# One kernel, 2,842 operations, another written-out order: fused sliding-window attention and gated MLP on one core

## The chip, the cores and the metric

One core of one Trainium2 chip runs the whole program. The metric is the device time of one execution in microseconds; the time of the kernel before is the median of its runs. The profile is a separate execution of the same program with the hardware profiler on; its own time is given below beside its span.

## The reference

There are 8 batches, 8 heads, 576 positions and 64 elements per head. Attention looks back over a window of 128 positions, with a bias that falls linearly with distance and a slope for each head. Its output, 4,608 tokens of 512 elements, goes through an MLP whose gate is `h * cos(h)`.

```python
scores = scale * np.matmul(q, k.transpose(0, 1, 3, 2))
bias = slopes[:, None, None] * (-np.abs(rel).astype(np.float32))[None, :, :]
mask = (rel >= 0) & (rel < window)                      # window = 128
scores = np.where(mask, scores + bias[None], -1000000000.0)
attn = softmax(scores)                                  # written out in the original
x = (attn @ v).transpose(0, 2, 1, 3).reshape(4608, 512)
h = x @ w_in                                            # 512 -> 2048
out = (h * np.cos(h)) @ w_out                           # 2048 -> 512
```

## The kernel before

**Stages.** The tokens are handled in nine chunks of 512 (the phases 0 to 8). Attention of the first batch comes ahead of them, as the opening part; the attention of the other batches is spread over the phases 0 to 5, between the matmuls of the MLP. The chunk of phase 0 is computed in two halves of 256 tokens (`moe1_half`, L975 to L984), the later ones in whole chunks (`moe1`, L782 to L791) or, from phase 6 on, by a seven-product scheme of block sums (`moe1_fast`, L876 to L943; the second matrix, L1067, uses such a scheme from phase 1 on). Those block sums are made by VectorE: `w_sums` and `w_in_sums` from the weights, `x_sums` from the tokens.

**One attention unit** is a pair of heads and 256 queries, or the 64 queries of the tail for all heads. Its steps are: `scores` (TensorE, L529 and L539), `exps` (ScalarE, L590 and L598), `mask` (VectorE, multiplies by the table `emask` of bias and window, L611 and L623), `pv` (TensorE, L640 to L656), `norm` (VectorE, a reciprocal L694 and a product L696), and `x_pe`, which transposes the result on TensorE (L742) and copies it to `xT` by ScalarE (L752) or VectorE (L753). In phases 2 to 5 some results go to `xT` by a transposing DMA instead (`x_dma`, L762 and L768, on SyncE's queue).

**The opening part.** The first 256 rows of q come by SyncE's queue into `ob` and are cast by VectorE and ScalarE (L367, L368). The first rows of k, and the second rows of both, come by Pool's queue (`load_qk`, L356). `qk_transposes` turns them on TensorE (L483): for each of q and k one block from the first rows (32 transposes for both) and one from the second rows (40 for both). Each block leaves two halves in PSUM, in two banks, and each half is copied to the tiles `qt` and `kt` by ScalarE (L500) or VectorE (L501). `masks` makes `emask`: eight exponentials on ScalarE, one for each head (L460), and four copies on VectorE (L465), each of which needs two of them.

**Later batches.** q and k of batch 1 come by `load_qk` as well. From batch 2 on `load_nat` (five DMAs each on Pool's queue, L385) brings them to `qnat` and `knat`, and `dma_transposes` (two transposing DMAs each on SyncE's queue, L396 and L399) turns them. `load_v` brings v in five blocks of rows for each batch (L375); `load_w_in` and `load_w_out` bring the weights in four parts each (L407, L413). All of these are on Pool's queue.

**What sets the order.** The program first makes a list of 2,842 operations with the tiles that they read and write. A packed table then gives one order of all of them; each engine runs its own operations in that order, and the table also names the engine for each copy that ScalarE or VectorE could do:

```python
for lo, hi in zip(raw[:n], raw[n:]):
    at = (at + lo + 256 * hi) % 65536
    o = self.all[at % 32768]
    if isinstance(o.fn, dict):
        e = "dve" if at >= 32768 else "act"
        o.fn, o.eng = o.fn[e], (e,)
    self.order.append(o)
```

Waits on semaphores follow from the list and the order (`emit`): an operation waits for the last one on each other engine or queue that it depends on. Nothing is reordered when the program runs. An operation that waits therefore holds up whatever stands behind it on its engine; on Pool and SyncE these are the issues of DMAs.

Of the kernel before, what the change touches and what calls it, by code (L numbers as in the profile page):

```python
# [8 lines left out]
ALU = mybir.AluOpType  # L9
# [21 lines left out]
    'c-nPV2Y6If7JmPfH!Wo*A%PHdEHqifjs=k}tV#(GFqBXPBn4$bu`FK_%_4*%1ObV(K#D*JSt&-E!h-'  # L31
    '0xDvPKfD@{Z`QYO7kX6D^JciMYzU|;fHUhcd1+;jf_Kj&N_3_w#jJy552L+3%Pc;zlP#H-yktj(-'
    'pEjqM{ck}PJwCrB3q-'
    '{9M;&d$5qHR9WADS}~;_2H1xbO#`q+wdtgon`B>6%HyG|f?3%VnDsdnr<5N0St5ZZ)?8zmXNGD<Zg2=y6N`U+Gy?'
    '$F$*GyJWJoN!r+3anTS_iMU&FrmJy)q1{k##U*rYHRJHq^Dy35b!Y@oPU}o$A?_9;n<O%5Xs0l2&{m^^1BgNm_9P'
    '~pqObs4C1TN&{Qy{6(86~%nA#%H5NW^O=4`d2vLnc~h(_}2&mQcz_^`@$G{b79x#rnLjt-93Hcj0-'
    'yv%|m2e+*e0cZK}!+72b)WUaJT8@pXD+fk0N6bOV1gB(Si4?NA5T2-'
    '!JB(zEKr!Mj%{>;HUNYjab!Z7$qCql;L3G!CjefR+FFk(bw73vr<2ntCbb8MB)_5dQYyf6J%<J=0tY;ul(MgN&rc'
    'O0s&EiG$uIcm#Y~Vab;v#yqnaVrE7GY>V-A}Btqa`;P_Nv&jvF#{*7WM`>VMkre&#)Wy?uO_aV#gax-'
    'm{4=v5trFP6j>R?Tw2c0rY#J*M(j<PaOY>o)>#w^hUa2)xJ2kX>J~-'  # L40
    '#3SczLYEI#)13`0UMgZCvSU&r@KXVhQx8AYHOt^~S#t385v1pL)39f1&X4(!RY_VSn%~;N7Le~0Vt5k)3C!7qncH'
    'Sb_KKyP6<WQBL=(H{om`}^2hwehkBNkN1f6-'
    '=6Jf`#n1*9F&|{#~8ip5b`?XFO3>mnmKg4fqM&X#D2BXTu`vb#MxEL-'
    '2=FZh<=U!>)?uhVjo~ev?pC0h90j^d!W2#$W>Vg}3Lez;yMB~`dF58D5!*GHZ4bkokcrZJo8XMBIs3+J`c0!*&!='
    'cNak2M(+9t6%k<c;_TI5&xT-;_~SjMe)zLQ?kr-'
    '9G)}so_oZgT~!nS)>B%(>F{i(nL<%Kma6dPT_kIY8xqVGm@6sSZY)QY;}3kyZHF!JjrNbPWohF6A1kpQae^Jz>4Y'
    'nMq|4ag_#Z%abX$X0Qx{bdg5-'
    'w!C^Sy0wzSSv6YO*7!5g5KOZPW>L)jeqDWi^PVfHiNt_&bV&I7<#pb?el1f*R3lvbBscPqQM6(|M=#E!7MQtWiEo'
    '^$q8jetWg{{laSk`ID;w6<lHL!It@CI3ZRWxET-dy=6bdfZi^BN)-'
    'kx6rkxYh^Af7Y$CX%W0qP@nf!;+_cuy#JAV$$(>L5)aS8M@n1a32RRL3Yb{W0a`!VJ8|o4{JEnxs(L});p(&v8a9'  # L50
    'u_yO{KZHL$YuW?tu(Sy-'
    '!vCGTmAdZpg4wXLtycpkG<<E5@OtDZg=!_1h1+Njmjw*z0aL)7QnhFOPv(elHPlI>oe%EXgvk}suL+RHI+l!oPEe'
    'ttc)y)KY7q-'
    'GO9HpEp~!82*s>_!_J5TR{@5f%EL7h^Wh(4l4fbO%j~jd783&`#My06C4>3;+Is6L%3tT|^hYe#$tr1&iB&6{dwW'
    'wmj!;Baz_4=p8Jja_9ps>tY{=<;GUvOwSAXGq+K`;>!KNrH|ImXY(ASTzHFN^apdvpSj*r6^VK)$8H@P=`NPcPO&'
    'XkYSBhFw`irt0gqb!LQPqlVQC7VwU?z)4yP6n<)+6xUk=rH29r)HJ=#nkkufV0J5o_@v9wsQWd0@&P$WT0e*0vOC'
    'WIl=#9la*x}LDtWaQG=0xl2(#f%Kz3QWi+K|tR$xwKh#_K~ywPUk>V_~X988-'
    'dL$7M*|kTUzrMQ~>ttJm@GYT>9QFLiQ#JGHIu^Q5UX9joXGsV+1N~s5tf4rg&Z0t843@yK)VUZ;eO{vvf>bj#_<{'
    'E{YJE13lG{)N}UY3D6Y>lsCkRX4ja{$9_e$IQETy;j`zD56VwIGwJ{vRRhIkkY72;<?OL;WxyDsbjLJ`d?#gik4L'
    '%OwvOj>3X-Yk5pe`ia}jeHouYwjx-lYe?zUO*6w~{=z!E<7?VOdoJcyIBk3;YN22T&Udsl*?z2EoT*eN`VQ(2lOw'  # L60
    '$ie!%Cd#CND}y^H-5G~apWoVM#%(x$>q1=4UeA7@v$>FHVpXpRNz-`z1w9-2S&rNI|0<^yIkuIxJ1&2qr-'
    'yn-P&*BAkwbEg<YgZWM`B<Ux7!?;yxT0hEB9Poq9_H<xB+6$<+&1*V*jXQ=!i##UhbBC-HxJ9b4f>O5FQM$GVlYY'
    '0;EzOMeT$+Oi@ir?~G>em;QF`Fb7Uw0-'
    ')DSUv5QX5E;wvHsQX@ok50m+CO*%wR0XM0gH$JNq(o?|pd}rcrfU%@Ny^NS$EwY}9WNlRrb}CwAb0!CyUIkX8zeE'
    't`lBMNi5`Z9289jS-byN0#8`Z0-K46!6u51NJvfI*I<pVOKD}#Bep<(EjKAJ>#OvyA?}aT-'
    'Eb<QtZWG>gAiq@nZu|-Z>5YIIxXgTPJ-Qv8(%8OF{x~utj?J<T~4~q=Mu!G!`B%o{U^X7EYfMjy|cFw5l`KlR}P!'
    'Ka8_mW<8uzKs|eA|5Ic*_e7cdlcU3q+K^v!GU5I4-4igxj^A<ASLge=;<iQSZL!w7=WR?W#-'
    'vXhCLeN@7x(>g+{qRDABl6lLS<Fw>!h`LQKaFe(HMu)ipAva=P&;AW;|7_8}?>Xa&1&CWqRI3oTyJm0VHkMj~b-'
    'KU~R;VLVn(IO$x|2XD-#Cwa~YvoxGM@0FUnOnlZXB(9|3jhMQu{ARUV7(DVnyPJ@o)_f&pP-'
    '0v1&I@q5tK0fHEZqW2B6vpePz;Nsr3p!)OwvLraMQ%IB0%b!Fk8kvD!^ICX(d5SU`>)JBl;A)3x!^A~*gA1H!Njk'  # L70
    '9bb31AJ#9jLnSFn5nJP8V+>6WI*{{9$K=-'
    'Ii4(}ekB>9rlTbz8;dAV@$vsGY#Mm*p3)v9cI)0mEeyn;9Sk1Ej+_{IEB=6m(OWM%qp|L4FkV=POcUwRSz4?%tjO'
    '!EE7%nJVFo1y$1xLEKDW3+%V*`a_(LEi!<eA{Ja22J?)4@RI|7PRIIN8a6UkTIrQNx^0MmIX}Gdse33v8*ibI3(}'
    'Q6!`hQq7VFL0TWDyL%1z)LEb|Fqa2QJsRyz<9M$)jGC(Gyq6mu#GUiIyWiMn}lrw_vC^2CnX65Kq(JOA5auqsW#('
    'az6gPr;3Fs3vS*iFTO!lleCE-fW~K`s@;f-'
    'DuL7*vWwMFvwo)YDYK%Ys!&lL=}a$qa_Dqe_$j$%4|P%7Sk&C^p7|E-05OoaEoQU{w(_HKhuIl)N)0L6E?If-ndQ'
    'f>bOkomPRMj6=zXYB;2Fs8S$=8>KAS9bxj%$jo92RQykW$_h$ynL-'
    ';1n|B~0C{NjJ5M;#~HD{_qDyS92ASr8Q=(}$hf?wlN8Dh7U35CEE3Rb4eZHcVrLB=YO&ys+EVM&F9-'
    '>_E|awkyN8>TE$>Y^ZLfm%hXRv?#4)t*Y5EYzr4%5w1xWK3uw7gWYn<tfyI;9|8HRZ>;#t145fwkp%W<gb}oO8Vt'
    ';%~TDI391Zd3iT@kVuEmcuME+!AOkCeh?Xh408{MGRAGcvK=>2_;SOCz;Xi5FXBMh@##BcNK~)Hu608vNLvl*BDH'  # L80
# [172 lines left out]
def bass_alibi_sliding__then__act_gcu_kernel(  # L253
# [8 lines left out]
    with ExitStack() as ctx:  # L262
# [966 lines left out]
        for u in range(1, 4):  # L1229
            load_w_in(u)  # L1230
            if u == 1:
                load_v(0, range(NBLK - LORD, NBLK))
# [92 lines left out]
```

## Time and profile before

| what | value |
|---|---|
| median of 3 runs | 299.79 us (299.76 to 300.42) |
| the profiled execution's own time | 299.71 us |
| its span in the profile | 298.0 us |
| granted TensorE clock | 1.0 |

The span reaches from the first to the last instruction of the profile; 1.71 us of the profiled execution's time lie around it. Lines beginning with a time in the quoted timelines are merged: the first number is the start, the second the length from the first to the last instruction of the group, and "x4" says how many there are.

### The profile page before, as it was taken

How to read it: one execution, taken by the hardware profiler on the slowest of the kernel's cores; microseconds unless marked ns; L12 is line 12 of the kernel's file. 1: busy time of each engine (PE TensorE's matmuls, PEld its weight loads, DVE VectorE, ACT ScalarE, POOL GpSimd, SP SyncE). 2: the span in 40 equal slices, each digit the busy share in tenths (PEclk: the TensorE clock that was granted, in tenths of full speed). 3: DMA queues.
4: the chain of work that ended last, by engine and by line, in shares of the span. 5: the costliest groups of instructions: out<-in, count | busy, mean ns of one | idle time of the engine just before them, and what ended most of it. 6: DMA issues, size and time to landing. Idle time of an engine off the chain costs nothing.

```text
span 298.0 us, 7278 instructions
## 1 busy us (share of the span) xinstructions
PE 287.9 (97%) x2974; PEld 205.2 (69%) x2974; DVE 262.1 (88%) x522; ACT 222.1 (75%) x318; POOL 95.2 (32%) x122
## 2 busy tenths in 40 slices
PE   2899999999999999999999999999999999999996
PEld 2678845446874586458854788547768888888884
DVE  3879877599977999899999999999999999999972
ACT  5788878689757889688777878579778758778620
POOL 7997000599642303991195005000000000000000
PEclk9999999999999999999999999999999999999999
DMA  7999999999999994999999939973131400041033
GB/s 153 173 205 208 207 169 146 180 196 155 136 175 147 130 187 90 142 173 173 169 170 133 163 85 130 159 164 74 21 79 21 150 2 0 2 141 37 10 134 106
DMA packets 147729, 37.96 MB, mean 127 GB/s; under 512 B 133360, under 2 KB 146416, under 8 KB 147696
## 3 DMA queue, kind: packets, MB, share of 16 engines
q0 software_dynamic: 99344, 18.10, 79.7%
q1 hardware_dynamic: 48352, 19.41, 34.5%
q8 instruction: 23, 0.38, 0.5%
q14 instruction: 10, 0.08, 0.1%
HBM read 36.70 MB, written 9.44 MB: 155 GB/s over the span
## 4 chain that ended last, share of the span: by engine, by line
PE 94%; DVE 2%; POOL 1%; issue 1%; ACT 1%; POOLq 0%; DVEq 0%
PE ps L1067 33%; PE ps L782 24%; PE ps L876 11%; PE ps L539 5%; PE ps L975 5%; PE ps L1161 4%; PE ps L653 3%; PE ps L656 2%; PE ps L742 2%; PE ps L483 2%; PE ps L529 1%; DVE kt L501 1%; PE ps L640 1%; PE ps L642 1%; PE ps L1138 1%
## 5 line engine op out<-in xcount | busy, mean ns | idle before, releaser
L1067 PE MATMUL ps<-w_outb,gT 128*128 128x256 f16 x512 | 82.3, 273 | 0.0
L782 PE MATMUL ps<-xT,w_inb 128*128 128x512 f16 x336 | 82.2, 379 | 0.0
L787 ACT ACTIVATE cos<-ps,halfpi 128x512 f32<-128x512 f32 x84 | 54.9, 687 | 18.9 <-PE ps L782 13.9
L598 ACT ACTIVATE p<-ps 128x768 bf16<-128x768 f32 (+1 forms) x64 | 55.6, 915 | 11.5 <-PE ps L539 9.5
L791 DVE TENSOR_TENSOR gT<-ps,cos 128x512 f16<-128x512 f32 x84 | 54.5, 686 | 5.5 <-ACT cos L787 5.1
L1067 PEld LDWEIGHTS ps<-w_outb,gT 128*128 128x128 f16 x512 | 48.2, 98 | 12.5 <-issue 1.3
L782 PEld LDWEIGHTS ps<-xT,w_inb 128*128 128x128 f16 x336 | 31.7, 98 | 31.1 <-DVE gT L791 1.5
L375 POOL DMA_DIRECT2D vp<-in_v_dram x40 | 34.3, 892 | 53.1 <-PE ps L656 35.3
L1067 PE MATMUL ps<-wsum,gsum 128*128 128x256 f16 x256 | 38.5, 273 | 0.0
L623 DVE TENSOR_TENSOR p<-p,emask 128x768 bf16<-128x768 bf16 (+1 forms) x64 | 38.0, 615 | 0.3
L385 POOL DMA_DIRECT2D qnat<-in_q_dram x30 | 25.5, 918 | 23.9 <-DMA qt<-qnat 23.9
L1052 ACT ACTIVATE ob<-ps 128x512 f32<-128x512 f32 x33 | 19.6, 598 | 13.7 <-PE ps L1067 11.2
L385 POOL DMA_DIRECT2D knat<-in_k_dram x30 | 25.7, 948 | 9.3 <-DMA kt<-knat 7.0
L1067 PEld LDWEIGHTS ps<-wsum,gsum 128*128 128x128 f16 x256 | 23.2, 98 | 4.0 <-issue 0.5
L876 PE MATMUL ps<-xT,w_inb 128*128 128x256 f16 x132 | 24.8, 273 | 0.0
L696 DVE TENSOR_TENSOR xnats<-ps,rec 128x256 f16<-128x256 f32 x56 | 21.9, 420 | 0.5
L539 PE MATMUL ps<-qt,kt 64*128 64x128 bf16 (+1 forms) x320 | 20.1, 253 | 1.3 <-DVE kt L501 1.3
L653 PEld LDWEIGHTS ps<-vp,p 128*128 128x128 bf16 x256 | 16.0, 99 | 4.3 <-issue 1.0
L653 PE MATMUL ps<-vp,p 128*128 128x65 bf16 x256 | 18.9, 196 | 0.1
L1067 PE MATMUL ps<-wsum,gT 128*128 128x256 f16 x112 | 18.1, 273 | 0.0
L539 PEld LDWEIGHTS ps<-qt,kt 64*128 64x128 bf16 x320 | 11.9, 98 | 8.6 <-issue 3.6
L1161 PE MATMUL ps<-w_outb,gT 128*128 128x512 f16 x64 | 17.6, 380 | 0.0
(111 smaller groups left out, 478.0 us busy)
## 6 DMA issues: line engine op xcount, KB each, us to landing
out_dram<-ob SPq DMA_DIRECT2D x35, 256.0 KB, 2.7
vp<-in_v_dram POOLq DMA_DIRECT2D x32, 128.0 KB, 6.9
qnat<-in_q_dram POOLq DMA_DIRECT2D x24, 128.0 KB, 7.1
knat<-in_k_dram POOLq DMA_DIRECT2D x24, 128.0 KB, 10.8
w_inb<-in_moe_w_in_dram POOLq DMA_DIRECT2D x4, 512.0 KB, 10.5
w_outb<-in_moe_w_out_dram POOLq DMA_DIRECT2D x4, 512.0 KB, 21.8
gsum<-in_q_dram POOLq DMA_DIRECT2D x1, 576.0 KB, 15.5
gsum<-in_k_dram POOLq DMA_DIRECT2D x1, 576.0 KB, 17.6
```

The costliest lines, as they stand in the source:

```text
L375: op("pool", [lambda e, t=t, rows=rows: e.dma_start(vp[b % 2][0:rows, t, :, 0:64], v[b, :, 128 * t:128 * t + rows, :].rearrange("h p d -> ...
L385: fns.append(lambda e, t=t, rows=rows: e.dma_start(nat[which][b % 2][0:rows, t, :, :], src[b, :, 128 * t:128 * t + rows, :].rearrange("h p ...
L539: ins = e.matmul(ps[:, banks[x], c0:c1], keys_ap(b, x, pr, kc), query_ap(b, x, pr, qb, 128 * nb), start=c0 == 0 and (b, pr, G) not in seed ...
L598: op("act", lambda e: e.activation(P[i][:, :, 0:hi], src_[:, :, 0:hi], ACTF.Exp, scale=0.125), w=held + [("P", i)], occ=920 if G else 691, ...
L623: op("dve", lambda e: e.tensor_tensor(p, p, m, ALU.mult), r=[("EM", h0), ("EM", h1)] + ([] if G else [("EM2", h1)]), w=[("P", i)], occ=600 ...
L653: ins = e.matmul(o, P[i][:, x, d0:d0 + 128], V[:, kc, h, 0:65], start=True, stop=not two)
L782: op("pe", lambda e, kc=kc: e.matmul(ps[:, bank, :], w_in[:, kc, 128 * fc:128 * fc + 128], xT[:, kc, r0:r0 + CH], start=(kc == 0), stop=(k ...
L787: op("act", lambda e: e.activation(cosb[ci][:, :], ps[:, bank, :], ACTF.Sin, bias=halfpi[:, 0:1]), r=["halfpi"], w=[("B", bank), ("cos", c ...
L791: op("dve", lambda e: e.tensor_tensor(gT[gi][:, fc, :], ps[:, bank, :], cosb[ci][:, :], ALU.mult), r=[("cos", ci)], w=[("B", bank), ("g", ...
L876: op("pe", lambda e, i=i, kc=kc: e.matmul(ps[:, bank, 256 * i:256 * i + 256], left(kc, p0 + i), right(kc), start=(start and i == 0 and kc ...
L1067: op("pe", lambda e, t=t, p=p: e.matmul(ps[:, bank, 256 * t:256 * t + 256], left(p, slice(128 * t, 128 * t + 128)), right(p), start=(start ...
L1161: op("pe", lambda e, t=t, fc=fc, bank=bank: e.matmul(ps[:, bank, :], gT[gi][:, fc, 128 * t:128 * t + 128], w_out[:, fc, :], start=(fc == 0 ...
```

## The change

The table is another one. No operation is added or taken away, none computes anything else, and the four settings and branches that are new in the text (`PCOS`, `LORD == 3`, and the choice of a group's name in `op`) are not active: `PCOS` is False and `LORD` is 0.

```diff
 TABLE = (
-    'c-nPV2Y6If7JmPfH!Wo*A%PHdEHqifjs=k}tV#(GFqBXPBn4$bu`FK_%_4*%1ObV(K#D*JSt&-E!h-'
...
+    'c-nPV30ze57M^bwhFMr<7^T$QEz8o<a>=as{FPaT3#KNbB8pE%)AtN2H6bm0F1e(MlA2-)YA7zzs`;`q$t-'
...
 )
-        f = fn[0] if isinstance(fn, list) else fn["act"] if isinstance(fn, dict) else fn
+        f = fn[0] if isinstance(fn, list) else next(iter(fn.values())) if isinstance(fn, dict) else fn
...
+        PCOS = False
...
-                op("dve", lambda e: e.tensor_tensor(o, srcs, cos, ALU.mult),
-                   r=r + ck, w=w + gk(hf), occ=1139, lat=1225, pri=MPRI, two=hf == 1)
+                f = lambda e: e.tensor_tensor(o, srcs, cos, ALU.mult)
+                if hf and PCOS:
...
+                else:
+                    op("dve", f, r=r + ck, w=w + gk(hf), occ=1139, lat=1225, pri=MPRI,
+                       two=hf == 1)
...
+        if LORD == 3:
...
+        else:
             distances()
             identity()
             load_qk("q", q, 0, 1)
```

Unpacked, the two tables give these orders. Of the operations on each engine, this many stand at another place in its sequence: 1,497 of 1,860 on TensorE, 115 of 304 on ScalarE, 326 of 522 on VectorE, 49 of 70 on Pool, 60 of 86 on SyncE. Fourteen copies change their engine, seven each way.

```
Pool, opening part (b0, b1: batches; "rows 2": the second rows of batch 0)
before: k rows 1 | distances 1 | q rows 2 | distances 2, 3 | k rows 2 | identity 1, 2 |
        v b0: 1, 0, 3 | w_in 0 | v b0: 2 | w_in 1, 2, 3 | q b1, k b1 | v b0: 4 | w_out 0-3
after:  k rows 1 | q rows 2 | distances 1 | identity 1 | distances 2 | identity 2 | k rows 2 |
        distances 3 | v b0: 1, 0, 3, 2 | w_in 0, 1, 2, 3 | v b0: 4 | q b1, k b1 | w_out 0-3

ScalarE, opening part (E: an exponential of masks, by head)
before: E2 E6 | cast q | E3 E0 E1 E5 | q copy a | k copy a | E4 E7 | exps 0, 1 | q copy d |
        exps 2, 3 | exps 4 5 6 | x copies 0, 2, 3 | exps tail, 7 | x copy 5 | cosines ...
after:  cast q | E6 | q copy a | E3 E1 E7 E0 E4 E5 E2 | exps 0, 1 | q copies c, d |
        exps 2, 3 | exps 4 5 6 | x copies 1, 2, 3 | exps tail, 7 | cosines ...

VectorE, opening part (a, b: halves of the first block, c, d: of the second)
before: memsets | cast q | q copy b | emask copy | k copy b | emask copies x3 | mask 0, 1 |
        q copy c | k copies d, c | mask 2, 3 | norms 0, 1 | norms 2, 3 | x copy 1 | ...
after:  memsets | cast q, memsets | q copy b | k copy a, k copy b | emask copies x2 | mask 0 |
        emask copy | mask 1 | emask copy | k copies d, c | mask 2, 3 | norms 1, 0 | norms 2, 3 | ...
```

TensorE's own order up to the first matmul of w_in is the same in both, but for the places of the four x transposes among themselves. The tail `pv` of batch 0 (L640) moves from behind the last matmuls of w_in of phase 0 to the first half of that phase. One of the sums of `w_sums` (0.68 us) moves, in phase 0, from ahead of the masks of the attention to behind the second pair of them. Further on, the loads and transposes of the last batches stand like this:

```
Pool, end of its list (b6, b7: batches)
before: v b6: 1 | q b7 | v b6: 2, 3 | v b5: 2 | v b6: 0 | k b7 | v b7: 3, 0 | v b6: 4 | v b7: 2, 4, 1
after:  v b6: 3 | k b7 | v b6: 4 | v b7: 0 | v b6: 2, 0 | v b5: 2 | v b6: 1 | v b7: 3, 1, 2, 4 | q b7

SyncE, the same stretch (x: x_dma with the number of its buffer, xt: of a tail, st: store)
before: ... st2 | transposes q b7 | st3 | x7 | xt1 | transposes k b7 | x2 | st0 | st1 | x6 | x0 | x1 | x5 | st2 ...
after:  ... st2 | transposes k b7 | x6 | x0 | transposes q b7 | st2 | st0 | xt1 | x4 | x5 | x2 | x7 | x1 | xt0 ...
```

More of the change, by code (lines that the diff above doesn't have):

```diff
@@ L38 @@
[L38 to L66, printed above, removed]
```

123 lines of the change are left out of this document (84 added, 39 removed).

## The prediction

> **What bounds the kernel now.** I read the page first, then the busy time in stretches, then the timeline of the opening part. Of the page, three lines:
>
> ```profile
> span 298.0 us, 7278 instructions
> ...
> PE 287.9 (97%) x2974; PEld 205.2 (69%) x2974; DVE 262.1 (88%) x522; ACT 222.1 (75%) x318; POOL 95.2 (32%) x122
> ...
> PE 94%; DVE 2%; POOL 1%; issue 1%; ACT 1%; POOLq 0%; DVEq 0%
> ```
>
> TensorE is busy for 97% of the span, and 94% of the chain that ended last is TensorE. The change adds no operation, so it can only gain or lose where TensorE waits. The busy time by stretches (after the stretch its length, then the engines in the order of the page) says where that is:
>
> ```profile
> 5.70:18.00 12.30, 11.03 (x161) 8.53 (x162) 10.35 (x26) 10.43 (x19) 12.30 (x17) 1.00 1.53 184
> 18.00:38.90 20.90, 20.90 (x269) 16.94 (x269) 17.63 (x35) 17.72 (x26) 10.97 (x13) 1.00 1.23 206
> 38.90:70.00 31.10, 30.96 (x250) 15.47 (x250) 23.97 (x53) 23.84 (x37) 14.81 (x18) 1.00 1.96 169
> ```
>
> TensorE idles 1.27 us in the opening part, nothing in phase 0, and 0.14 us in the next 31 us. Of its 10.1 us of idle time, 5.70 lie ahead of the first transpose (below). So the opening part decides, and afterwards only new waits can count. (Busy matmuls overlap in the profile, so a wait of 0.2 us can hide in a busy stretch; I come back to that.) The opening part, from the timeline:
>
> ```profile
> 4.88 0.63 ACT L368 ACTIVATE gsum<-ob 128x512 bf16<-128x512 f32 x1
> ...
> 5.70 1.92 PE L483 MATMUL ps<-ident,gsum 128*64 128x128 bf16 x32 [5.70 <-POOL ident L421]
> 6.81 0.60 ACT L500 ACTIVATE qt<-ps 128x512 bf16<-128x512 bf16 x1
> ...
> 7.66 0.60 ACT L500 ACTIVATE kt<-ps 128x512 bf16<-128x512 bf16 x1 [0.26 <-PE ps L483]
> 7.66 0.69 DVE L501 COPY kt<-ps 128x512 bf16<-128x512 bf16 x1
> 8.15 0.71 ACT L460 ACTIVATE emask<-dif 128x256 bf16<-128x256 f32 x2
> ...
> 8.50 0.82 PE L539 MATMUL ps<-qt,kt 64*128 64x256 bf16 x8 [0.88 <-DVE kt L501]
> ...
> 9.04 1.51 ACT L598 ACTIVATE p<-ps 128x768 bf16<-128x768 f32 x2 [0.17 <-PE ps L539]
> ...
> 9.25 2.35 PE L483 MATMUL ps<-ident,gsum 128*64 128x128 bf16 x40
> ...
> 10.57 0.88 ACT L500 ACTIVATE qt<-ps 128x640 bf16<-128x640 bf16 x1
> ...
> 11.79 1.57 DVE L501 COPY kt<-ps 128x640 bf16<-128x640 bf16 x2
> ...
> 13.26 1.02 DVE L623 TENSOR_TENSOR p<-p,emask 128x768 bf16<-128x768 bf16 x2
> ...
> 14.47 0.34 PE L653 MATMUL ps<-vp,p 128*128 128x65 bf16 x3
> ...
> 15.64 0.76 DVE L696 TENSOR_TENSOR xnats<-ps,rec 128x256 f16<-128x256 f32 x2
> 15.83 1.22 PE L742 MATMUL ps<-ident,xnats 128*128 128x128 f16 x8
> ...
> 17.96 0.94 PE L975 MATMUL ps<-xT,w_inb 128*128 128x256 f16 x7
> ```
>
> The two halves of k leave PSUM side by side at 7.66, one on ScalarE, one on VectorE; TensorE's scores wait for the later one, 0.15 us after its end at 8.35.
>
> **The opening part, step by step.** *Start.* TensorE starts at 5.70, released by Pool's identity; ScalarE's cast ended only just before, at 5.51. In the new order the identity comes earlier, ahead of the second rows of k, and the cast decides: TensorE waits 0.15 for such a copy (at 8.35, above), so it starts at 5.65 to 5.70, at most 0.05 us earlier. *k.* Both halves of k are now copied by VectorE, one behind the other: 7.66 to 8.35, and the second some 0.6 later, to 8.94 (two q copies of 640 in the row at 11.79 take 1.57, so the second begins 0.1 before the first ends). The first scores go from 8.50 to 9.09: **+0.59**. *Masks.* ScalarE spends what it saves on the exponentials: two take 0.71, so one each 0.31. The old order did two of the eight ahead of the cast, where ScalarE now waits; the new one does seven behind the q copy, from 7.3 to 9.5. The exps of the first scores, ready at 9.6, find ScalarE just free: +0.6 as well, nothing more. *Second block.* TensorE's 40 transposes shift to 9.85. Their first half is done at 11.13, and now ScalarE copies both q halves, 0.88 each, 0.1 overlapped: 11.17 to 12.82. VectorE, which has one copy less, does the two k halves as soon as the last transpose ends (12.2): until 13.81 instead of 13.36, **+0.45**. The next exps follow the q copies, 12.71 to 14.22 by the 1.51 of the pair; the second mask (0.56, as two take 1.02) ends at 14.81 instead of 14.28, and the second `pv` starts at 14.99 instead of 14.47: **+0.52**. *x.* The second of the two norms behind it ended at 16.40, 1.93 after the start of `pv`; so now at 16.92. Before, the last two pairs of x transposes stood behind that norm, in the new order only the last pair does; so their end moves less, from 17.05 to 17.36: **+0.31**. From there on all is TensorE's own pace: the first matmul of w_in goes from 17.96 to some 18.26, less the 0.05 of the start: **+0.25**. Both ends: zero, if the waits further on take up all of it; +0.59, if the serial copy goes through whole. I take 0.25, the sum.
>
> *Loads.* The third block of v and w_in's first part change places; two rows of landing times stand for them:
>
> ```profile
> 8.90 0.92 POOL L375 DMA_DIRECT2D vp<-in_v_dram  x1
> ...
> DMA to landing us min/median/max: 8.0/8.0/8.0
> ...
> DMA to landing us min/median/max: 7.9/10.5/13.2
> ```
>
> The first belongs to that block (landed at 16.9), the second to w_in's four parts, whose first is issued at 8.15 and lands at 16.05. Exchanged, w_in's first part lands no later than the pair did before, at 16.9, 1.3 us ahead of its first matmul; the block of v, needed behind that matmul, was not waited for. Worth zero both ways. The cover is those 1.3 us: a landing later than 18.2 would cost what it is late.
>
> **Phase 0 and after.** The x copy that stood behind the last exps on ScalarE is now VectorE's. These rows are ScalarE's way from the exps to the cosines:
>
> ```profile
> 18.99 1.02 ACT L598 ACTIVATE p<-ps 128x1024 bf16<-128x1024 f32 x1
> ...
> 21.26 1.28 ACT L980 ACT_TABLE_LOAD   x1
> ...
> 22.55 1.27 ACT L980 ACTIVATE cos<-ps,halfpi 128x512 f32<-128x512 f32 x2
> ```
>
> The load of the table can begin at 20.1 instead of 21.26, and the first cosine at 21.4. That wins room for ScalarE and VectorE, nothing on TensorE, which idles 0.00 in this stretch. In return the new order brings the first bank's next tile forward: TensorE reaches it 35 matmuls (0.11 each), two `pv` of 0.49 and two x transposes behind 18.25, at 23.25; the product that frees the bank ends at 22.8. VectorE then goes through its products at 0.6 each and frees the banks of the third and fourth tile at 25.45 and 26.1, when TensorE comes at 25.44 and 26.0. Such waits of 0.1 us I count at **+0.15** in all (0 to 0.4). Against that, one of the sums over the weights of L1067 (128x1024 like VectorE's at L623, 0.6) leaves VectorE's way ahead of the masks in the chain of waits; then a row of the page:
>
> ```profile
> 47.62 1.20 DVE p L623 x2
> ...
> 48.98 0.18 PE ps L653
> ...
> 49.62 1.08 PE ps L1161 x5
> ```
>
> ```profile
> L1161 PE MATMUL ps<-w_outb,gT 128*128 128x512 f16 x64 | 17.6, 380 | 0.0
> ```
>
> The `pv` at 48.98 starts 0.16 behind the end of its mask, at TensorE's usual distance, so it waited. Five matmuls of 0.38 take 1.08 there, 0.22 each: their ends overlap by 0.16, and so much of a wait does not show as idle time. With the 0.14 us of idle time in the stretch I put what goes at **-0.2** (0 to -0.4, were a second such wait freed too). From 70 us on the operations on TensorE, ScalarE and VectorE stand in almost the same groups, pairs exchanged; I see no wait that goes or comes for certain and take zero, ±0.5.
>
> **Sum:** 0.25 + 0.15 - 0.2 = +0.2 us. The profiled execution took 299.71, so 299.9 like it; that is 0.08 under the median of 299.79, and the forecast for the median is **300.0**.
>
> **The rivals.** *q of batch 7 comes last (slower).* Its load now stands at the end of Pool's list, behind four blocks of v that can only go at 178; then SyncE's transposes wait for it, with stores and x transposes queued behind them. Pool's blocks, the landing of k's five pieces of batch 7 beside other transposes, SyncE's transposes of k alone, four x transposes, their landing, VectorE's sum of x, its masks, and the `pv` that needs them:
>
> ```profile
> 178.20 4.88 POOL L375 DMA_DIRECT2D vp<-in_v_dram  x6 [17.81 <-PE ps L539]
> ...
> DMA to landing us min/median/max: 8.8/10.8/12.8
> ...
> 191.15 2.90 SPq L396 DMA_TRANSPOSE kt<-knat  x1
> 194.09 1.59 SPq L399 DMA_TRANSPOSE kt<-knat  x1
> ...
> 198.15 5.52 SPq L768 DMA_TRANSPOSE xT<-xnats  x4
> ...
> 205.50 0.42 DVE L843 TENSOR_TENSOR xsum<-xT 128x512 f16<-128x512 f16 x1
> ...
> 206.44 1.11 DVE L623 TENSOR_TENSOR p<-p,emask 128x768 bf16<-128x768 bf16 x2
> ...
> 207.98 0.26 PE L653 MATMUL ps<-vp,p 128*128 128x65 bf16 x3
> ```
>
> Four blocks at 0.8 and five pieces at 0.9 put the last issue at 185. Landing 8 us later, at 193, lets the transposes end at 197.5; two stores (0.6 each) and five x transposes (1.3 each) later, at 205.2, the one that the sum of x needs is issued, and it lands by 206.3. VectorE reaches the sum at 206.8, as a 0.69 sum and one of the masks now precede it: no wait. At 10.8 us, the middle of the row, it is 2.8 us later: VectorE waits 2.3 us, less some 0.4 that the `pv` has in hand: up to +1.9. It decides from a landing at 193.5. I take the middle, +1.0: **301.0**. For it: in this kernel loads beside transposes were that slow. Against: fewer transposes are queued then.
>
> *A table switch costs more than its load (slower).* If something as long again followed it, the first cosine would come at 22.7, the product that frees the first bank end at 24.2, and TensorE wait from 23.25 to 24.35 where it had 0.4 in hand: +1.1, **301.1**. The row at 21.26 speaks against: 1.28 us later, at 22.55, the cosine runs. [...]
>
> *Nothing of the serial copy is taken up (slightly slower).* +0.59 - 0.05 instead of +0.25: **300.3**.
>
> *More waits go than come (faster).* VectorE and ScalarE, 1.1 us ahead after the opening part, spare TensorE hidden waits between 28 and 70 us, of the 0.2 above each, at copies, masks and norms. Room for them there is: the chain gives VectorE and ScalarE 3% of the span, 8.9 us, and the opening part's pieces do not fill that. Six such waits are what I would grant: -1.2 instead of -0.2, no new ones, and the +0.25 stays: **298.8**.
>
> *The order changes nothing that TensorE feels*, in the opening part either: **299.8**.
>
> **How the numbers follow.** Forecast 0.36, copy not taken up 0.10, no effect 0.06, q of batch 7 0.26, table 0.02, more waits gone 0.20. About 0.3%, 0.9 us, is what a measurement of this kernel can tell. Faster than 298.9: 0.20. Slower than 300.7: 0.26 + 0.02 = 0.28. Between: 0.52. The range goes from 298.6, the fastest case with one more of its waits of 0.2 gone, to 301.6; of the slow case, which ends at 301.9, the last part is left out.
>
> **What would show it.** Right: k copies on VectorE at 7.66 and 8.3, first scores near 9.1, first matmul of w_in at 18.1 to 18.4, first cosine near 21.4. Wrong: w_in before 17.9; or TensorE idle near 208 with SyncE's transposes of q starting after 194; or a wait of TensorE for VectorE in phase 0 of over 0.3 us.

## The result, and the profile after

The changed kernel takes 303.24 us (median of 4 runs, 302.55 to 305.15) against 299.9 us for the kernel before (median of now 4 runs, 299.76 to 300.42): the ratio is 1.0121, with a 95% interval of 1.0095 to 1.0148. I had forecast 300.0 with a range of 298.6 to 301.6; the result lies outside, on the side of the rival "q of batch 7 comes last". The profiled execution took 302.55 us, the shortest of the four, with a span of 300.8 us against 298.0. Its mean granted clock was 1.0, that of the other three 0.994; the last section comes back to that.

From the page of the changed kernel: the span, the engines' busy time, and the chain that ended last, by engine.

```profile
span 300.8 us, 7282 instructions
...
PE 287.4 (96%) x2974; PEld 203.9 (68%) x2974; DVE 261.0 (87%) x522; ACT 222.5 (74%) x318; POOL 95.0 (32%) x122
...
PE 83%; DMA 6%; SPq 3%; POOL 2%; DVE 2%; ACT 1%; issue 1%; POOLq 0%; DVEq 0%; ACTq 0%
```

TensorE is as busy as before (287.4 against 287.9 us), so in this execution its work did not become slower; something waits. The chain, 94% TensorE before, now spends 9% of the span, some 27 us, on transfers (DMA) and on SyncE's queue (SPq). Where, the busy time in stretches tells (stretch, its length, then the engines in the order of the page):

```profile
5.70:18.00 12.30, 9.81 (x160) 7.46 (x160) 10.05 (x28) 10.67 (x20) 11.89 (x16) 1.00 1.53 181
18.00:38.90 20.90, 20.90 (x274) 17.02 (x267) 18.04 (x40) 17.03 (x27) 13.05 (x16) 1.00 1.23 206
38.90:70.00 31.10, 31.06 (x253) 15.52 (x252) 23.80 (x51) 24.56 (x38) 12.32 (x15) 1.00 1.95 169
205.00:215.00 10.00, 7.76 (x97) 5.76 (x97) 7.25 (x16) 6.07 (x8) 0.00 (x0) 1.00 0.26 62
```

In the last of these TensorE idles 2.24 of 10 us. In the kernel before it idled not at all there:

```profile
205.00:215.00 10.00, 10.00 (x149) 7.64 (x147) 9.71 (x20) 8.05 (x11) 0.00 (x0) 1.00 0.18 43
```

(The first stretch shows more idle time than before, 2.49 against 1.27 us, and yet ends at the same time; that belongs to TensorE's pace, in the last section.) The chain of waits through that place, in order of time (start, length, what):

```profile
178.18 3.32 POOL vp L373 x4
181.50 0.88 POOL qnat L383
...
184.93 10.73 DMA qnat<-in_q_dram
195.67 1.92 SPq L394
...
197.64 1.67 SPq L397
...
204.69 1.37 SPq L766
...
206.11 3.54 DMA xT<-xnats
...
209.73 0.13 DVE xsum L841
...
210.07 0.56 DVE p L621
...
210.77 0.25 PE ps L651 x3
```

Read from the top: Pool issues four blocks of v, then q of batch 7; its last piece is issued at 184.93 and lands 10.73 us later. Only then can SyncE's two transposes of q go. Behind them on SyncE's queue stand two stores and transposes of x; one of them, that of buffer 7, starts at 206.11 and lands 3.54 us later. VectorE's sum of x needs it, VectorE's next mask stands behind the sum, and TensorE's `pv` needs the mask. Two rows of the waits and the rows of VectorE and TensorE give the sizes:

```profile
SPq L394 <- DMA qnat<-in_q_dram: 7.0, 1, 7.0
```

```profile
209.73 0.42 DVE L841 TENSOR_TENSOR xsum<-xT 128x512 f16<-128x512 f16 x1 [2.69 <-DMA xT<-xnats]
```

```profile
210.77 0.25 PE L651 MATMUL ps<-vp,p 128*128 128x65 bf16 x3 [2.24 <-DVE p L621]
```

SyncE stands still for 7.0 us, VectorE for 2.69, TensorE for 2.24 and, with the 0.16 by which its matmuls there overlap (0.27 long, 0.11 apart), 2.4. Ahead of this place the two kernels are at the same point of TensorE's work to within 0.5 us.

The opening part, for the steps of the sum:

```profile
5.65 1.92 PE L481 MATMUL ps<-ident,gsum 128*64 128x128 bf16 x32 [5.65 <-ACT gsum L366]
9.05 0.82 PE L537 MATMUL ps<-qt,kt 64*128 64x256 bf16 x8 [1.48 <-DVE kt L499]
...
14.94 0.27 PE L651 MATMUL ps<-vp,p 128*128 128x65 bf16 x3
...
17.70 0.41 PE L527 MATMUL ps<-qt,kt 64*128 64x64 bf16 x16
18.04 0.94 PE L979 MATMUL ps<-xT,w_inb 128*128 128x256 f16 x7
```

```profile
6.11 3.52 POOL L373 DMA_DIRECT2D vp<-in_v_dram  x4 [1.07 <-DVE vp L441]
```

The first scores start at 9.05 (8.50 before), the second `pv` at 14.94 (14.47), w_in at 18.04 (17.96). Pool's loads of v, and all behind them, start 0.6 us later than before (5.51), since Pool waits 1.07 us for a memset which now stands behind VectorE's cast.

### The profile page after: what moved, and what is told of

It reads as the page before. It is cut to its first block, busy times and chain, and to the rows that moved or that the text cites. A ratio compares the mean times of both kernels' runs of the same rounds, so it can differ in the third digit from the quotient of the medians.

```text
span 300.8 us, 7282 instructions
## 1 busy us (share of the span) xinstructions
PE 287.4 (96%) x2974; PEld 203.9 (68%) x2974; DVE 261.0 (87%) x522; ACT 222.5 (74%) x318; POOL 95.0 (32%) x122
## 4 chain that ended last, share of the span: by engine, by line
PE 83%; DMA 6%; SPq 3%; POOL 2%; DVE 2%; ACT 1%; issue 1%; POOLq 0%; DVEq 0%; ACTq 0%
PE ps L1071 29%; PE ps L780 20%; PE ps L874 11%; PE ps L979 5%; PE ps L1165 5%; PE ps L537 4%; DMA qnat<-in_q_dram 4%; PE ps L651 3%; PE ps L654 2%; PE ps L481 1%; DMA ob<-in_q_dram 1%; PE ps L740 1%; SPq L766 1%; DMA xT<-xnats 1%; POOL vp L373 1%; ACT p L596 1%
## 5 line engine op out<-in xcount | busy, mean ns | idle before, releaser
L1071 PEld LDWEIGHTS ps<-w_outb,gT 128*128 128x128 f16 x512 | 48.0, 98 | 12.1 <-issue 1.3
L537 PE MATMUL ps<-qt,kt 64*128 64x128 bf16 (+1 forms) x320 | 19.4, 247 | 2.2 <-DVE kt L499 1.8
L651 PE MATMUL ps<-vp,p 128*128 128x65 bf16 x256 | 18.6, 195 | 2.5 <-DVE p L621 2.2
L654 PE MATMUL ps<-vp,p 128*128 128x65 bf16 x192 | 17.3, 194 | 0.0
```

The source lines that it names most:

```text
L537: ins = e.matmul(ps[:, banks[x], c0:c1], keys_ap(b, x, pr, kc), query_ap(b, x, pr, qb, 128 * nb), start=c0 == 0 and (b, pr, G) not in seed ...
L651: ins = e.matmul(o, P[i][:, x, d0:d0 + 128], V[:, kc, h, 0:65], start=True, stop=not two)
L654: ins = e.matmul(o, P[i][:, x, p0:p0 + 128], V[:, kc - 1, h, 0:65], start=False, stop=True)
L1071: op("pe", lambda e, t=t, p=p: e.matmul(ps[:, bank, 256 * t:256 * t + 256], left(p, slice(128 * t, 128 * t + 128)), right(p), start=(start ...
```

## The experiments

Orders are given as the lists of the change are: parts that are struck or added, all else in place. "The old order" is that of the kernel before, "the new order" the changed one. A table of all medians follows the experiments.

**Is the late load the loss?** Four kernels: the load earlier; the load late, but two transposes of x ahead of q's; and the two halves of the change.

```diff
 Pool:  ... v b6: 1
+q b7
 v b7: 3, 1, 2, 4
-q b7
```

> One load is moved in the changed order: q of batch 7 goes ahead of the four blocks of v of batch 7 on Pool's list, so its first piece is issued at about 159.6 (Pool idles there until 178.18) and not at 181.4. Nothing else moves. Theory (the late load is the whole loss): it lands by 175, SyncE's transposes of q no longer wait, VectorE's sum of x at 206.8 finds its data, TensorE's wait of 2.24 us at 210.77 goes, and the time is 300.0 to 300.4. Rival (the loss is spread over the new order, the late wait only shows some of it): over 301.5. Rival (another load, now behind q, becomes the late one): one of the v blocks or the next x transposes show a new wait of TensorE between 178 and 215 of over 0.5 us.

300.6 us, 1.0016 of the kernel before (1.0001 to 1.0031). Some 2.6 of the 3.3 us are gone, not all (what the granted clock has to do with the 3.3 stands in the last section). The load is issued at 160.10 and lands at 176.78; VectorE waits for no transfer between 195 and 220; its sum of x follows on the mask at once:

```profile
207.13 0.56 DVE L618 TENSOR_TENSOR p<-p,emask 128x768 bf16<-128x768 bf16 x1
207.61 0.42 DVE L838 TENSOR_TENSOR xsum<-xT 128x512 f16<-128x512 f16 x1
```

But the profile has two other waits of TensorE for data, at 20 and 143 us, which come up again below. The "DMA" row is the landing of w_in's second part, and "issue" a wait whose releaser the profile does not name; `pv` starts there 0.09 behind the landing of a block of v:

```profile
PE ps L648 <- issue: 0.6, 1, 0.6
PE ps L976 <- DMA w_inb<-in_moe_w_in_dram: 0.3, 1, 0.3
```

The second kernel leaves the load late:

```diff
 SyncE: ... transposes k b7 | x6 | x0
+xt1 | x7
 transposes q b7 | st2 | st0
-xt1
 x4 | x5 | x2
-x7
 x1 ...
```

> The load of q of batch 7 stays at the end of Pool's list and lands late, at about 195.7. On SyncE's list two transposes of x (buffer 7 and the second tail), which the sum of x needs, move from behind the transposes of q of batch 7 to ahead of them. Theory (what costs is what stands behind the waiting transposes on SyncE, not q itself): SyncE still waits some 4 to 5 us for q, but x lands by 195, the sum starts at 206.8 without a wait, and the time is 300.0 to 300.5. Rival (q itself is late): TensorE or VectorE waits for q's transposes near 207, and the time stays at 302 to 303. Rival (the transfers are slow there whatever their order): the two x transposes still land after 207, over 301.5.

300.32 us (1.0011, 0.9998 to 1.0024). Here q lands nearly as late as in the changed kernel, at 194.94 against 195.66, and SyncE still waits:

```profile
SPq L391 <- DMA qnat<-in_q_dram: 4.2, 1, 4.2
```

VectorE's sum, however, runs without a wait, behind the mask as in the run above:

```profile
206.16 0.56 DVE L618 TENSOR_TENSOR p<-p,emask 128x768 bf16<-128x768 bf16 x1
206.64 0.42 DVE L838 TENSOR_TENSOR xsum<-xT 128x512 f16<-128x512 f16 x1
```

So q itself, landing at 194.94, was not too late for TensorE. The loss is what stands behind the waiting transposes on SyncE's queue.

The halves, cut at about 150 us:

```diff
-order = new
+order = old[:1400] + [o for o in new if o not in old[:1400]]     # the one: new tail
+order = new[:1400] + [o for o in old if o not in new[:1400]]     # the other: old tail
```

> The old order up to about 150 us, the new order from there on: the last batches' loads, transposes and attention in the new order, behind the old opening part and phases 0 to 3. Theory (late load): 302.3 to 303.5, with TensorE's wait for the mask near 210 of 1.5 to 3 us. Rival (the new opening part costs about 0.3 to 0.6 of the loss): 302.0 to 302.7 here. Rival (the loss comes from the earlier part): 299.8 to 300.3.

301.88 us (1.0089, 1.0056 to 1.0122), with the wait of the changed kernel: the load lands at 196.35, and

```profile
DVE xsum L838 <- DMA xT<-xnats: 2.7, 1, 2.7
```

This profile is of one of the two long executions of the five (303.8 us), in which the granted clock fell as well (last section); the median is of those at full clock.

> The other half: the new order up to about 150 us, the old one from there on. It prices the new opening part and phases 0 to 3 alone. Theory (late load is all): 299.8 to 300.1, the profile shows first scores at 9.05 and TensorE's lag gone by 20 us. My prediction's sum for this part: 300.0 (+0.25 +0.15 -0.2). Rival (the serial copy is paid in full): 300.4. Rival (the new first part is a gain): under 299.5.

300.74 us (1.0041, 1.0019 to 1.0064): the first half costs too, more than the 0.2 that my sum gave it. Its profile has the two waits of the first experiment, at 20.58 and 143.74, and in this run w_in's first part landed at 18.02, so that TensorE's first matmul of w_in (18.07) waited for it. The two halves together, 1.9 and 0.75 against the 299.99 us of the kernel before beside them, make 2.65 us. That is what the one execution of the changed kernel at full clock lost (302.55 against 299.9); the median's other 0.7 comes in with the executions at 0.994.

**How late is too late?** The changed kernel with one load two places earlier:

```diff
 Pool:  ... v b7: 3, 1
+q b7
 v b7: 2, 4
-q b7
```

> The changed kernel with q of batch 7 behind two of the four blocks of v of batch 7 and not behind all four; nothing else moves. Its first piece is issued at about 179.8 instead of 181.45. Theory (the loss goes with the landing, one for one, above 193.1 or so): it lands about 1.65 us earlier, at 194.0, VectorE's sum of x waits about 1.0 us instead of 2.69, and the time is 301.4 to 302.0. Rival (the transposes of k on SyncE's queue, issued from 179.8 on, set the landing, not the issue): it still lands at 195 to 196 and the time stays at 302.5 to 303.5.

301.4 us (1.0041, 1.0026 to 1.0057), at the low end. The first piece is issued at 180.34 and the load lands at 193.22, 2.4 us before that of the changed kernel; SyncE waits 4.1 us, VectorE and TensorE not at all at this place, where a wait of 1.0 us was expected. So the time in the expected span is partly luck: the profiled execution took 300.40 us, a full 1.0 under the median, and whether the longer ones had a later landing is not shown. With landings at 195.66 and 196.35 VectorE waited 2.7 us; so the point from which the load costs lies between 193.2 and 195.7, and 193.5, as the rival had it, fits.

**The other loads.** The wait at 20 us is for w_in's second part, the one at 143 for block 3 of v of batch 4 (the expectations on record name it batch 5, and say that it goes ahead of four loads, where the list below shows seven; the block is the one at "L648", issued at 127.05 and landed at 142.60 in the changed kernel, 139.39 before). Both kernels here have q of batch 7 early.

```diff
 VectorE: memsets
+memset v (64x256)
 cast q | memsets
-memset v (64x256)
```

> The new order with q of batch 7 early (as in the first experiment), and one memset of VectorE (64x256, the zeros of v's first buffer) ahead of its cast of q. In the changed kernel Pool's first block of v waits 1.07 us for that memset, and every load behind it is issued later: w_in's second part at 10.34 where it was 9.78. That part landed at 18.79, 20.22, 19.83 and 20.54 in four profiles of the new first part, where TensorE wants it at about 19.85. Theory (that memset delays the loads): v's first block is issued at about 5.05, w_in's second part at about 9.3, it lands at 18.8 to 19.5, TensorE does not wait for it, and the time is 0.2 to 0.5 under that of the first experiment (300.6): 300.1 to 300.4. Rival (the queue's bytes set the landing, not the issue): it still lands between 19.5 and 20.5, and the time is 300.5 to 300.7.

300.6 us (1.002, 1.0007 to 1.0033): nothing gained. Pool's loads of v do start at 4.97 and w_in's second part is issued at 9.19, but it lands at 20.05, and TensorE waits:

```profile
20.10 1.16 PE L976 MATMUL ps<-xT,w_inb 128*128 128x256 f16 x9 [0.31 <-DMA w_inb<-in_moe_w_in_dram]
```

The rival's numbers came: an issue 1.1 us earlier did not bring this landing forward. That the bytes ahead in the queue set it, as the rival has it, is not shown by this. The wait for the memset, 1.07 us of Pool, cost nothing that this run can tell.

```diff
 Pool:  ... k b5
+v b4: 3
 q b6 | v b5: 0 | q b5 | v b5: 1, 3 | v b4: 4 | k b6
-v b4: 3
 (and the memset as above)
```

> As the run with the early memset, and besides the load of v of batch 5, block 3, goes back ahead of four loads on Pool's list (before q of batch 6, its old neighbour order). In the new order it landed at 142.3 to 143.7 and TensorE's pv at 142.4 to 143.7 starts 0.09 behind it; in the old order it landed at 139.4, three us early. Theory (a third late load): no wait of TensorE at 142 to 144, and 0.1 to 0.7 less than the run with the early memset: 299.6 to 300.0. Rival (the lag there is met again behind it, or another load takes its place): the same time as without this move, with a wait of over 0.2 between 120 and 150.

299.94 us (0.9995, 0.9984 to 1.0007): with three loads put back the new order is as fast as the old one. The block lands at 114.23 and there is no wait at 143. In this profile w_in's second part landed at 19.09, so that the 0.66 us to the run above are not this block's alone.

**The opening part.** The serial copy of k, undone alone:

```diff
 ScalarE: cast q | E6 | q copy a
+k copy a
 E3 E1 E7 E0 E4 E5 E2 ...
 VectorE: ... q copy b
-k copy a
 k copy b ...
```

> As the run with all three loads moved, and the first half of k's first block is copied by ScalarE behind its copy of q, as in the old order, and not by VectorE ahead of the second half. Theory (the serial copy of k is hidden behind the landing of w_in): first scores at 8.45 instead of 9.05, TensorE reaches w_in at about 17.5 and its second part at about 19.3, then waits for the landing: 0 to 0.2 us less than without it, 299.5 to 299.9. Rival (the copy costs its 0.59 or my 0.25 in full once the loads are early): 0.25 to 0.6 less. Rival (ScalarE's exponentials come late instead and the second half of the opening part is slower): 0.1 to 0.4 more.

301.21 us (1.0046, 1.0031 to 1.0062), 1.3 us slower than with the copy on VectorE: the third rival, at three times the upper end that it was given. ScalarE's rows with the copy on ScalarE, then the same rows of the run above:

```profile
7.59 0.60 ACT L495 ACTIVATE kt<-ps 128x512 bf16<-128x512 bf16 x1 [0.26 <-PE ps L478]
8.08 2.24 ACT L455 ACTIVATE emask<-dif 128x256 bf16<-128x256 f32 x7
10.22 1.49 ACT L593 ACTIVATE p<-ps 128x768 bf16<-128x768 f32 x2
11.60 1.55 ACT L495 ACTIVATE qt<-ps 128x640 bf16<-128x640 bf16 x2
```

```profile
7.08 2.24 ACT L455 ACTIVATE emask<-dif 128x256 bf16<-128x256 f32 x7
9.42 1.51 ACT L593 ACTIVATE p<-ps 128x768 bf16<-128x768 f32 x2
10.95 1.56 ACT L495 ACTIVATE qt<-ps 128x640 bf16<-128x640 bf16 x2
```

The first scores do come 0.46 earlier (8.42), but the exponentials of the masks and of the scores and q's second copies come 0.65 to 1.0 later, since in the new order all seven masks and both second copies of q are ScalarE's as well. The first `pv` starts at 13.41 instead of 12.77, and w_in at 18.64 instead of 17.64 (a part of that is TensorE's slow pace, last section: in this profile six matmuls of scores took 0.61 us at 16.47 and 0.40 at 17.98). That copy was the price of another exchange, and could not be judged alone.

The part of the change that its name tells, in the old order:

```diff
 Pool:  ... v b0: 1, 0, 3
-w_in 0
 v b0: 2
+w_in 0
 w_in 1, 2, 3 ...
```

> The old order with one edit, the part of the change that its name tells: v's third block (of batch 0) goes ahead of w_in's first part on Pool's list. Theory (the two only change places in the queue): w_in's first part lands at 16.5 to 17.0, its second part as before at 19.1 to 19.5, TensorE's first matmul of w_in stays at 17.5 to 18.0, the time is within 0.15 us of the kernel before: 299.8 to 300.1. Rival (each load behind is put back): the second part lands after 19.7 and the time is 300.2 to 300.6. Rival (a gain: v is there earlier and w_in's later parts too): under 299.7.

299.65 us (0.9993, 0.9979 to 1.0006): no change that can be told. w_in's parts land at 16.18 and 19.05.

Then both orders crossed: the old opening part (with that exchange) before the new rest with its loads put back.

```diff
+order = old[:109] + [o for o in new_3_loads if o not in old[:109]]   # 109: up to the first matmul of w_in
```

> The opening part in the old order, with v's third block ahead of w_in (as in the run of that edit alone), and everything behind the first matmul of w_in in the new order with its late loads put back (q of batch 7, v of batch 5 block 3). Against the run with the three loads it prices the new opening part; against the run with v's third block alone it prices the new order behind the opening part. Theory (the opening part is worth nothing either way, since both wait for w_in's second part at 19.0 to 20.2): 299.5 to 300.0, within 0.3 of both. Rival (the new opening part is slower by the 0.25 that I put down): 299.5 to 299.7 here against 299.94. Rival (the new order behind the opening part is faster by 0.2, as -0.2 in my sum has it): 299.3 to 299.5.

304.71 us (1.0162, 1.0132 to 1.0192; 302.65 and 302.66 in the two executions at full clock, 304.5 to 306.24 in the four at 0.994 and 0.989), but not for the reason under test: on Pool's list v's fifth block of batch 0 came in its old place, behind q and k of batch 1, while TensorE's tail `pv` came in its new one.

```profile
PE ps L635 <- DMA vp<-in_v_dram: 3.0, 1, 3.0
```

The block landed at 30.4; the wait is of the kind of the result's, a load that comes behind others and an operation that is brought forward. With w_in's second part ahead of v's third block as well:

> As the run with the old opening part and the new rest, and w_in's second part goes ahead of v's third block on Pool's list (it landed 0.9 us or more behind that block in each profile), with the first pv that needs this block put behind ten more matmuls of w_in on TensorE. Theory (the bytes ahead of w_in's second part set when TensorE can go on at 19 to 20): that part lands at 18.1 to 18.6, TensorE does not wait for it, the block of v lands at 19.0 to 19.4, just when its pv comes, and the time is 0.2 to 0.5 less: 299.1 to 299.5. Rival (the pv or what follows on VectorE and ScalarE becomes the late one): the same time or up to 0.5 more, with a wait of TensorE behind 20 us.

303.55 us (1.0134, 1.0101 to 1.0167), spoilt by the same load (1.7 us), and in its profile by a fall of the granted clock between 16 and 20 us (last section). Three runs mend it.

```diff
 Pool:  ... w_in 3
+v b0: 4
 q b1, k b1
-v b0: 4
```

> As the run with the old opening part and the new rest, but v's fifth block of batch 0 goes ahead of q and k of batch 1 on Pool's list, as the new order has it. Behind them it landed at 30.4 in that run, and the tail pv, which the new order brings forward to 27.2, waited 3.2 us for it; so that run did not show what it was meant to. Theory (the two opening parts are worth the same, both wait for w_in's second part): 299.5 to 300.1, no wait at 27 to 31. Rival (my -0.2 for phases 0 and 1 holds on top of the old opening part): 299.3 to 299.5. Rival (the new opening part is worth more than the old one): 300.2 to 300.6.

299.27 us (0.9983, 0.9969 to 0.9997): the lowest median of this study, 0.5 us (0.1 to 0.9) under the kernel before, and so under both. No wait of TensorE stands in its profile between 18.2 and 205 us.

```diff
 Pool:  ... v b0: 1, 0, 3
-v b0: 2
 w_in 0, 1
+v b0: 2
 w_in 2, 3 ...
 TensorE: the first pv of that block seven matmuls of w_in later
```

> As the run above, and w_in's second part ahead of v's third block, with the first pv of that block ten matmuls later on TensorE. Without the late fifth block it should show what the second run of this pair could not. Theory (the landing of w_in's second part sets the pace at 19 to 20): it lands at 18.2, TensorE does not wait for it, 0.2 to 0.5 less than the run above. Rival (TensorE's own slow pace up to 19 us, with w_in matmuls 0.21 apart instead of 0.11 as in the profile of that run, takes it back): the same time or up to 1 us more, with such matmuls between 17 and 19.

299.85 us (1.0006, 0.9996 to 1.0017). (The expectations say ten matmuls; in the lists it is seven.) w_in's second part lands at 18.13, early enough, and now the block of v lands at 19.21 and its `pv` starts at 19.25: the wait has changed its load.

> The same two moves (w_in's second part ahead of v's third block, the first pv of that block ten matmuls later) in the new order with its three loads put back. Theory (landing sets the pace): w_in's second part lands at 18.2 to 18.8 where it was 19.1 to 20.2, and the time is 0.1 to 0.5 under that run's 299.94: 299.4 to 299.8. Rival (in the new order VectorE and ScalarE, not the landing, are what TensorE waits for in the opening part): 299.9 to 300.2. Rival (pv later costs): over 300.2.

300.13 us (1.0016, 1.0006 to 1.0026): the block of v is waited for in the new order too (19.73 and 19.78). Here w_in's second part, though issued at 8.33, landed only at 19.38; so the theory, which had it land at 18.2 to 18.8, failed.

| kernel | median us | ratio (95%) | w_in's second part landed / first used |
|---|---|---|---|
| before | 299.9 | | 19.40 / 19.44 |
| changed | 303.24 | 1.0121 (1.0095-1.0148) | 18.79 / 20.07 |
| q b7 early | 300.6 | 1.0016 (1.0001-1.0031) | 20.22 / 20.26 |
| x7 ahead of the transposes of q | 300.32 | 1.0011 (0.9998-1.0024) | 19.83 / 19.87 |
| old, new from 150 us | 301.88 | 1.0089 (1.0056-1.0122) | 19.13 / 19.18 |
| new, old from 150 us | 300.74 | 1.0041 (1.0019-1.0064) | 20.54 / 20.58 |
| q b7 early, memset early | 300.6 | 1.0020 (1.0007-1.0033) | 20.05 / 20.10 |
| and v b4: 3 early | 299.94 | 0.9995 (0.9984-1.0007) | 19.09 / 19.66 |
| and k copy a on ScalarE | 301.21 | 1.0046 (1.0031-1.0062) | 19.14 / 20.67 |
| old, v b0: 2 ahead of w_in | 299.65 | 0.9993 (0.9979-1.0006) | 19.05 / 19.10 |
| q b7 two places earlier | 301.4 | 1.0041 (1.0026-1.0057) | 18.72 / 19.81 |
| old opening, new rest, loads put back | 299.27 | 0.9983 (0.9969-0.9997) | 18.87 / 19.48 |
| and w_in 1 ahead of v b0: 2 | 299.85 | 1.0006 (0.9996-1.0017) | 18.13 / 19.75 |
| new, loads put back, w_in 1 ahead | 300.13 | 1.0016 (1.0006-1.0026) | 19.38 / 20.27 |
| old opening, new rest, v b0: 4 late | 304.71 | 1.0162 (1.0132-1.0192) | 19.20 / 19.62 |
| and w_in 1 ahead of v b0: 2 | 303.55 | 1.0134 (1.0101-1.0167) | 18.16 / 20.70 |

## Why the prediction was wrong

The mechanism of the result was on record, step by step, as the rival with 0.26; the forecast had 0.36. In the sum, the term that failed is "From 70 us on": it was taken as zero, ±0.5, and at 208 to 211 us alone TensorE idled 2.24 us for the late load. What failed, by the prediction's own steps:

*"q of batch 7 comes last": right in the chain, wrong in its price and its chance.* I let the load land 8 us behind its last issue, at 193, and called 10.8, the middle of the row, the bad case; I took half of the loss because fewer transposes would be queued then. But 8 us is under the shortest of the row that I quoted (8.8/10.8/12.8): with the last issue at 185, all three of its values lie above the 193.5 from which the load decides. The last piece took 10.73 us, the middle. And of the x transposes I gave each 1.3 us on SyncE's queue and 1.1 more to land, 2.4 in all; the one that counted took 3.54. So VectorE waited 2.69 us where the far end of the rival had 2.3, and TensorE, with the overlap, 2.4 where it had 1.9. With that row as it stood the rival said 301.9, and it, not the forecast, was the likeliest. The load late with x ahead of it (300.32) shows that the place of the loss is SyncE's queue, as written.

*The loads of the opening part: the wrong part of w_in.* "w_in's first part lands ... 1.3 us ahead of its first matmul" held in most profiles (in one it landed at 18.02 and was waited for). But the second part is what TensorE stands at. Already in the trace of before it landed at 19.40 and was used at 19.44; I did not set the one beside the other. In the first twelve rows of the table it landed between 18.72 and 20.54, and in seven of them TensorE's first use came 0.04 to 0.05 behind the landing. So the opening part's gains and losses end at a landing that moves by 1.8 us from one profile to the next.

*A load that I did not look at.* v of batch 4, block 3, used at 142.5, landed at 139.39 before; three loads that now precede it (v b5: 0, v b4: 4, k b6) put the landing at 142.28 to 143.78 in six profiles with the new order there, always 0.09 ahead of its use. "From 70 us on ... I see no wait that goes or comes for certain" went by operations on TensorE, ScalarE and VectorE; Pool's list was compared only at its end.

*The serial copy of k: +0.59, then +0.25.* The first half was measured: 9.05, +0.55. For w_in, five profiles with the old opening part (17.96, 17.50, 17.27, 17.61, 17.47; mean 17.56) stand against seven with the new one (18.04, 17.78, 17.80, 18.07, 17.61, 17.64, 17.78; mean 17.82): +0.26, close to the +0.25 of the sum, though the pair of profiles of before and after has only +0.08. That it is so close is partly luck: within each group the profiles differ by 0.5 to 0.7, and without the profile of before, whose slow pace lasted to 17.8 us (last section), the old mean is 17.46 and the difference +0.36. What it is worth in time the landing above decides; the best kernel has the old opening part, but its interval overlaps that of the new one with its loads put back, so that isn't shown.

*Phases 0 and 1: +0.15 and -0.2.* The rest of the span behind the first use of w_in's second part, in the kernels without a late load, is 298.0 - 19.44 = 278.6 us (before) and 297.6 - 19.10 = 278.5 (v's block alone) for the old order, and 297.7 - 19.66 = 278.0 and 297.5 - 19.48 = 278.0 for the new one. But the new order has five more matmuls of w_in (0.11 each) ahead of that use, and they are the difference. So these terms were near nothing together, as their sum of -0.05.

*The other steps.* The first cosine came 1.30 behind the start of the table's load (20.33, 21.63), so the rival of the dearer switch fell:

```profile
20.33 1.28 ACT L984 ACT_TABLE_LOAD   x1
21.63 1.84 ACT L984 ACTIVATE cos<-ps,halfpi 128x512 f32<-128x512 f32 x3
```

The start at 5.65, released by the cast, was right to 0.05. The wait of Pool for the memset, which I had not seen, turned out to cost nothing (300.6 us with it and without it).

*The median above the profile.* The far end of the rival was 301.9; the profiled execution took 302.55, and the other three 0.5 to 2.6 us more, which puts the median at 303.24. The prediction had no term for that. All three have a mean granted clock of 0.994; the last section shows, in another kernel with the same wait, what such a reading went with. That the clock fell at the same place in these three is not shown, since they have no trace; landings that move, of three loads with no slack, may add to it.

## What to carry to other kernels

When an order changes, set for every load the landing of the old trace beside the first use in the new order, over the whole list, and treat a slack under the scatter of the landings (here 1 to 2 us) as a wait; a mean over rows, not the shortest, is the landing to expect. On an in-order queue of transfers ask of each entry that can wait what stands behind it: here a load that was not itself too late cost some 2.6 us through two transposes queued behind its transposes, and either moving the load or moving those two gave it back. Where the granted clock falls behind a wait of TensorE, the wait costs more than its length: in one profile here, with the clock at 0.72 and 0.50, the matmuls behind it took 4.03 us instead of 2.83. A copy moved between engines is judged with the copies that it was exchanged for.

## What the runs showed of the hardware that I had not expected

**TensorE had two paces in the opening part, and the moment of the change moved by some 5 us.** The same 16 matmuls of the tail scores in the kernel before and in the changed one (0.64 against 0.41 us), and the first matmuls of w_in in two other runs of this study (the one with three loads put back, then the spoilt one with w_in's second part ahead):

```profile
17.39 0.64 PE L529 MATMUL ps<-qt,kt 64*128 64x64 bf16 x16
```

```profile
17.70 0.41 PE L527 MATMUL ps<-qt,kt 64*128 64x64 bf16 x16
```

```profile
17.64 0.94 PE L976 MATMUL ps<-xT,w_inb 128*128 128x256 f16 x7
```

```profile
17.77 2.61 PE L976 MATMUL ps<-xT,w_inb 128*128 128x256 f16 x14
```

The matmuls of a `pv`, of 65 columns each, started 54 ns apart at the one pace (the second `pv` of the kernel before, 14.47 to 15.07) and 29 at the other (that of the changed one, 14.94 to 15.29), those of w_in 213 (the last row above) and 109 (the row ahead of it). In the profile of before the slow pace lasted to 17.8 us, in the changed one to 14.5, and in five others it had ended by the first `pv`, at 12.1 to 13.1; in the last row above it was fast at 14.3, slow again from 16 to 19, and fast after that. The granted clock of the views reads 1.00 in the first three of these stretches, at both paces, so in the opening part it is the distance of equal matmuls that shows the pace (the first clock record, of 1.0, begins at 17.93 us in the trace of the kernel before and at 14.55 in that of the changed one, within 0.15 us of the change of pace in each; ahead of it there is none). In the last row the fall is seen in that column too:

```profile
16.00:18.00 2.00, 1.74 (x28) 1.34 (x29) 2.00 (x5) 1.80 (x5) 2.00 (x4) 0.56 1.67 186
18.00:20.00 2.00, 2.00 (x13) 1.47 (x12) 0.63 (x2) 1.98 (x3) 2.00 (x3) 0.58 1.34 205
```

What sets the moment is not shown. In the trace of before the slow pace lasted through the second `pv` and the x transposes to the tail scores, which alone took 0.23 us more than in the changed kernel (0.64, 0.41). So a part of what looks like absorbed delay, +0.47 at the second `pv` but +0.08 at w_in, is the slow pace of the trace of before and not slack of the order.

**In one profile the granted clock fell behind a wait of TensorE.** In the profile of the kernel with the new order from 150 us on, TensorE waits 2.29 us for the mask, to 210.67, as in the changed kernel (2.24, to 210.77). Behind it the clock falls, which it does not in the profile of the changed kernel (last line):

```profile
210.00:212.00 2.00, 1.33 (x16) 1.11 (x17) 2.00 (x6) 0.00 (x0) 0.00 (x0) 0.72 0.25 46
212.00:214.00 2.00, 2.00 (x19) 1.14 (x17) 1.93 (x4) 0.29 (x1) 0.00 (x0) 0.50 0.44 124
```

```profile
212.00:214.00 2.00, 2.00 (x27) 1.65 (x27) 1.94 (x4) 1.19 (x2) 0.00 (x0) 1.00 0.38 108
```

The same matmuls up to the next `pv` take 4.03 us there (211.17 to 215.20) and 2.83 in the changed kernel (211.13 to 213.96). Of the five executions of that kernel, three have a mean clock of 1.0 and took 301.71 to 301.88 us, two have 0.994 and took 303.80 and 303.99. Of the 21 executions of the four kernels in which TensorE waits 1.7 us or more at one place (the changed one, this one and the two spoilt ones), 13 have 0.994 or less; of the 114 of the other eleven kernels of the experiments, 5. Why the clock falls in some executions and not in others is not shown, nor that the wait alone does it: in the second of the spoilt kernels the profile has the fall at 16 to 20 us, ahead of the wait at 28.5.

**Issuing a load earlier did not bring it in earlier here.** w_in's second part, at the same place of Pool's list but issued at 10.34, 9.19 and 9.20, landed at 18.79, 20.05 and 19.09. The gap between the landings of w_in's first and second part was 2.5 us in some profiles (18.79 - 16.30 in the changed kernel) and 3.5 in others with the same order (20.22 - 16.67 with q of batch 7 early). What takes that 1.0 us was not found.
